# Other parts for the last weights, f16 halves and an f16 selector for the slots' output, low centroid sums in PSUM, and all steps in another sequence

## The chip, the cores and the metric

One core of a Trainium2 chip runs the whole program. The metric is the device time of one execution in microseconds (us). A core has TensorE (matmuls and their weight loads), VectorE, ScalarE, GpSimd, and SyncE, whose queue issues most of the DMAs. In the profile these are PE and PEld, DVE, ACT, POOL and SP.

## The reference

Three stages in one launch, with results in float32 (w_in and w_out come in with 64 bits a value):

```
# 1. clustered attention: batch 2, 8 heads, 768 positions, head size 64, 16 clusters
q_assign = argmax(normalised q . normalised centroids);  k_assign likewise
scores = where(q_assign == k_assign, q @ k.T / 8, -1e9)
attn_out = softmax(scores) @ v                     # -> x: 1536 tokens x 512
# 2. a dense layer
h = x @ w_in                                       # 512 -> 2048
x = (h * clip(h + 3, 0, 6) / 6) @ w_out            # 2048 -> 512
# 3. soft mixture of experts: 8 experts, 4 slots each
logits = x @ phi                                   # 1536 x 32
slot_input = softmax(logits, over tokens).T @ x    # 32 x 512
slot_out[e] = relu(slot_input[e] @ w1[e]) @ w2[e]  # w1: 512 x 1024, w2: 1024 x 512
out = softmax(logits, over slots) @ slot_out       # 1536 x 512
```

w1 and w2 are 8 x 2 MB each, 32 MB that are read once.

## The kernel before, in words

**Steps.** The kernel is a list of 1178 small generators ("events"): each `yield` ends a step. The string `ORDER` is a list of event numbers; `flush` takes one step of an event for each number, and so writes the instruction stream of every engine. The program text fixes which steps there are, `ORDER` alone fixes their sequence on each engine and in each DMA queue. The string `ROOMS` gives many tiles the number of their buffer, in PSUM and SBUF.

**Attention.** For each of the 16 heads (`HEADS`): `load` brings q, k and v; `cast_hi` and `cast_lo` split q and k into f16 halves (high, and what is left, low) in one buffer that all heads share, and a transpose DMA turns them; `as_mm` multiplies with the high and low halves of the centroids (`ct`), adds both sums and begins the arg-max, `as_max` ends it, `as_put` puts the one-hot rows beside q and k; `maxq`, `maxr` and `shift` find each row's maximum; `scores`, `exps`, `plow` and `pv` make the weighted sums, and `finish` divides. `cnt_mm` is for clusters without keys. The halves of a product are summed in PSUM, so that f16 matmuls give float32 accuracy. For head 0 the turning is done by TensorE.

**Weights of the dense layer.** w_in and w_out come as 16 loads of 512 KB each (`win_load`, `wout_load`) in a wider format (64 bits a value), and are narrowed in place (`narrow`: two instructions on VectorE, L912 and L916, one on ScalarE) and then split. w_out is folded with phi (`wphi1` to `wphi3`) and written back to DRAM for the end.

**Dense layer.** `hid`, `act`, `logits`, `colmax`, `dweights` and `dispatch` run for 12 tiles of 128 tokens; those of the first batch lie between the attention heads of the second. At the end `zsum`, `slot_in` and `slot_t` make the slots' inputs.

**Experts.** `fetch` brings w1 and w2 in chunks of 1 MB, in the order of `chunks`, each into the room that `rooms` names; a room comes free when its last reader is done, and a load in SP's queue waits for that, with all behind it. `layer1`, `relu`, `turn` and `layer2` work on groups of four experts, of which each has 32 columns of TensorE. The second layer of the last group is made in two `PARTS` of the 512 output columns (`layer2_part`), so that the first part can go out while the weights of the second come: 384 columns and then 128. Their chunks are of kind "d". `slots_out` takes the 4 rows of each expert out of the group results (`o2s`, float32, copied from PSUM) with a selector matrix `sel` in float32, built by 24 small GpSimd copies, and splits the sum into f16 halves (`s16`); `combine` multiplies with the softmax weights, scales and writes out, in six DMAs for the first part and two for the second.

**Keep.** `keep` issues matmuls (L377) whose result nobody reads; 136 of them lie where TensorE would stand still.

## Time and profile before

| | us |
|---|---|
| median of 3 runs | 449.64 (448.59 to 452.29) |
| the profiled execution | 451.0 |
| its span, first to last instruction | 449.1 |
| TensorE busy | 429.5 (96% of the span) |
| ScalarE, VectorE, GpSimd busy | 309.8, 274.9, 251.1 |
| granted TensorE clock, mean | 0.991 |

Times below are us from the start of the span. Busy time of TensorE counts "keep" matmuls too, and matmuls that overlap in its pipeline.

### The profile page before, as it was taken

The page shows a single profiled execution, that of the slowest core. Times are in us where ns is not written, and L with a number is a line of the kernel's source. Part 1 is how long each engine was busy: PE and PEld are TensorE (multiplying, and loading weights), DVE is VectorE, ACT ScalarE, POOL GpSimd, SP SyncE. Part 2 cuts the span into 40 slices and gives each one's busy share as a digit, 9 for nine tenths or more (in the row PEclk, how much of TensorE's full clock was granted, in tenths as well). Part 3 has the DMA queues.
Part 4 walks back from the last instruction along what each step waited for, and adds up shares of the span by engine and source line. Part 5 has one row for each costly group of instructions (what it writes and reads, how often), then busy time and mean ns, then how long its engine had stood idle before and what let it go on. Part 6 is the DMA issues. An engine that isn't in the chain of part 4 may idle for free.

```text
span 449.1 us, 11732 instructions
## 1 busy us (share of the span) xinstructions
PE 429.5 (96%) x4866; PEld 276.1 (61%) x4866; DVE 274.9 (61%) x479; ACT 309.8 (69%) x508; POOL 251.1 (56%) x229
## 2 busy tenths in 40 slices
PE   8899999999999999999999999999999999889983
PEld 6567778777886556565656567774555445623432
DVE  5989999999866686484666577513434225540322
ACT  7789999988999887888778789874344344501112
POOL 6557588965665676678759788884232333130000
PEclk9999999999999999999999999999999999989997
DMA  8999958997677998407664719907996888799978
GB/s 268 250 201 221 262 89 230 232 234 257 223 173 108 273 260 190 140 14 153 131 165 86 175 22 341 227 14 143 290 393 183 200 216 273 249 378 347 382 211 278
DMA packets 126645, 95.23 MB, mean 212 GB/s; under 512 B 95360, under 2 KB 111744, under 8 KB 126592
## 3 DMA queue, kind: packets, MB, share of 16 engines
q1 hardware_dynamic: 122672, 88.69, 75.1%
q10 hardware_dynamic: 3920, 5.80, 3.6%
q8 instruction: 38, 0.62, 0.6%
q14 instruction: 15, 0.12, 0.1%
HBM read 64.06 MB, written 7.34 MB: 159 GB/s over the span
## 4 chain that ended last, share of the span: by engine, by line
PE 73%; DVE 11%; DMA 6%; ACT 5%; issue 2%; POOL 1%; SPq 0%; DVEq 0%; ACTq 0%; POOLq 0%
PE h L745 27%; PE st L591 5%; PE sm L553 5%; PE st L595 5%; DVE mxs L569 4%; PE acc L661 4%; PE acc L674 3%; DMA wk<-in_moe_w_dram 2%; PE acc L667 2%; PE acc L666 2%; DMA pr<-in_moe_w_dram 2%; PE z L853 2%; PE kw L377 2%; PE lg L796 2%; DMA qk1t<-pr 1%
## 5 line engine op out<-in xcount | busy, mean ns | idle before, releaser
L368 POOL TENSOR_TENSOR pp<-p,pp 128x768 f16<-128x768 f32 x72 | 118.4, 1653 | 46.6 <-ACT pp L358 31.7
L745 PE MATMUL h<-wq,xt 128*128 128x512 f16 x576 | 134.1, 379 | 0.0
L569 DVE TENSOR_REDUCE mxs<-sm 128x1 f32<-128x768 f32 x96 | 89.1, 951 | 20.7 <-PE sm L553 19.9
L745 PEld LDWEIGHTS <-xt 128*128 128x128 f16 x576 | 54.4, 98 | 59.4 <-issue 2.1
L368 POOL TENSOR_TENSOR ghl<-r,ghl 128x1024 f16<-128x1024 f32 (+1 forms) x25 | 50.3, 2014 | 59.1 <-ACT ghl L358 54.6
L639 ACT ACTIVATE p<-st 128x768 f32<-128x768 f32 x72 | 58.2, 811 | 18.3 <-PE st L595 14.4
L358 ACT ACTIVATE pp<-p 128x768 f16<-128x768 f32 x72 | 60.4, 842 | 2.8 <-PE acc L674 1.8
L764 DVE SCALAR_TENSOR_TENSOR r<-r,h 128x1024 f32<-128x1024 f32 (+1 forms) x26 | 29.5, 1137 | 28.6 <-ACT r L762 28.3
L762 ACT ACTIVATE r<-h,b_relu 128x1024 f32<-128x1024 f32 (+1 forms) x26 | 27.1, 1047 | 17.6 <-POOL ghl L368 9.4
L591 PE MATMUL st<-qk1t 128*128 128x384 f16 x144 | 35.1, 325 | 2.3 <-DVE qk2t L578 0.7
L358 ACT ACTIVATE ghl<-r 128x1024 f16<-128x1024 f32 (+1 forms) x26 | 25.5, 986 | 16.1 <-PE z L853 8.4
L667 PE MATMUL acc<-v,pp 128*128 128x64 f16 x432 | 36.1, 194 | 0.0
L666 PE MATMUL acc<-v,pp 128*128 128x65 f16 x432 | 36.1, 192 | 0.0
L661 PE MATMUL acc<-v,pp 128*128 128x65 f32 x288 | 35.6, 273 | 0.0
L661 PEld LDWEIGHTS acc<-v,pp 128*128 128x128 f32 x288 | 34.7, 192 | 0.9
L595 PE MATMUL st<-qk2t 102*128 102x384 f16 x144 | 35.2, 325 | 0.0
L553 PE MATMUL sm<-qk2t 80*128 80x384 f16 x144 | 34.4, 325 | 0.7 <-ACT wot L989 0.2
L666 PEld LDWEIGHTS <-pp 128*128 128x128 f16 x432 | 31.5, 99 | 2.9
L368 POOL TENSOR_TENSOR pr<-pr,pr 128x768 f16<-128x768 f32 x15 | 25.2, 1677 | 13.6 <-ACT pr L358 10.3
L667 PEld LDWEIGHTS <-pp 128*128 128x128 f16 x432 | 29.2, 96 | 2.8
L358 ACT ACTIVATE pr<-pr 128x768 f32<-128x768 f32 (+2 forms) x32 | 26.3, 823 | 4.0 <-DMA qk1t<-pr 2.2
L377 PE MATMUL kw<-ident,ident 128*128 128x256 f16 x136 | 22.9, 294 | 2.6 <-POOL b_relu L870 1.7
(223 smaller groups left out, 801.7 us busy)
## 6 DMA issues: line engine op xcount, KB each, us to landing
wk<-in_moe_w_dram SPq DMA_DIRECT2D x36, 512.0 KB, 6.7
wi<-in_moe_w_in_dram SPq DMA_DIRECT2D x16, 512.0 KB, 6.2
wod<-in_moe_w_out_dram SPq DMA_DIRECT2D x16, 512.0 KB, 4.8
pr<-in_moe_w_dram SPq DMA_DIRECT2D x12, 512.0 KB, 6.5
wos<-wo ACTq DMA_DIRECT2D x8, 512.0 KB, 3.3
wk<-wos SPq DMA_DIRECT2D x8, 512.0 KB, 5.1
pr<-in_q_dram SPq DMA_DIRECT2D x16, 192.0 KB, 4.4
pr<-in_k_dram SPq DMA_DIRECT2D x16, 192.0 KB, 4.3
```

The source lines that it names most:

```text
L358: nc.scalar.activation(out, in_, AF.Copy, scale=scale)
L368: (nc.vector if e == "v" else nc.gpsimd).tensor_tensor(out=out, in0=in_, in1=hi, op=ALU.subtract)
L377: nc.tensor.matmul(t[:, 0, 0:256], ident16, ident.bitcast(F16), start=True, stop=True)
L553: nc.tensor.matmul(s[:, j, 0:384], d["qk2t"][0:80, n, 0], d["qk2t"][0:80, 3 * j : 3 * j + 3, 1], start=True, stop=True,)
L569: nc.vector.tensor_reduce(out=mxs[i % 2][:, 96 + n : 97 + n], in_=s[:, :, 0:384], op=ALU.max, axis=AX.XY)
L591: nc.tensor.matmul(s[:, j, 0:384], d["qk1t"][:, t, 1], d["qk1t"][:, 3 * j : 3 * j + 3, 0], start=True, stop=False)
L595: nc.tensor.matmul(s[:, j, 0:384], d["qk2t"][0 : 96 + NT, t, 1], d["qk2t"][0 : 96 + NT, 3 * j : 3 * j + 3, 0], start=False, stop=True,)
L639: nc.scalar.activation(p32, s[:, :, 0:384], AF.Exp, scale=sc_exp)
L661: nc.tensor.matmul(o, p32[:, j, r * P : (r + 1) * P], d["v32"][:, t], start=(t == 0 and n == 0), stop=False)
L666: nc.tensor.matmul(o, hi, v1[:, t, 0:65], start=(t == 0 and n == 0), stop=False)
L667: nc.tensor.matmul(o[:, 0:64], hi, v1[:, t, 65:129], start=False, stop=False)
L745: nc.tensor.matmul(s[:, fb % 2], xt[:, lhs], wq[fb][:, hl, kk], start=(n == 0), stop=(n == 11))
```

## The change

There are five edits:

- `as_mm`: for heads 0 and 1 the sums with the low centroids are added in PSUM by 24 matmuls of 16 columns, in place of 12 of 32 columns, a copy on ScalarE and an add on VectorE. The other 14 heads stay as they were.
- `PARTS`: 352 and 160 columns in place of 384 and 128. The chunks "d" are cut anew: for each of the four experts four loads of two rows of 352 columns each for part 0, in two chunks, and two of four rows of 160 columns for part 1; all loads of part 1 stand behind all of part 0.
- The group results leave PSUM as two f16 halves (`o2_halves`: the high one by ScalarE, the low one by VectorE), scaled by a mask of each group's rows; the selector is f16, made by one GpSimd copy of `i4`.
- `slots_out` multiplies the high halves into rows 0 to 64 and the low ones into rows 64 to 96, and the two copies of the result are one of ScalarE and one of VectorE.
- `ORDER` and `ROOMS` are new throughout. The loads of w_in and the steps on them stand at other places; the warm-up of the Exp table (`second`) stands later; fourteen `keep` events stand behind the last `act` where eight stood before.

The diff, without the strings of `ORDER` and `ROOMS`, of which 179 lines are changed:

```diff
--- before.py
+++ after.py
@@ -27,179 +27,179 @@
 ORDER = (
-    "0 837 807 9 811 8 9 809 0 15 15 803 829 840 0 0 0 16 16 16 16 16 5 10 8 11 13 13 842 848 834 820 8 8 16 16 8 "
...
+    "9 0 9 822 838 13 836 8 0 810 811 15 15 1124 8 823 7 13 12 12 16 16 842 16 16 8 63 16 110 829 16 837 0 832 16 "
...
@@ -463,21 +463,29 @@
         d = st[i]
         pm = psm(f"as_{i}")
         a2 = pm[:, 0 : 24 * C].rearrange("p (n l c) -> p n l c", l=2, c=C)
+        a = a2[:, :, 0]
         for n in range(2 * NT):
-            nc.tensor.matmul(
-                a2[:, n],
-                d["qk1t"][:, n // 2, n % 2],
-                ct[:, :, h * C : (h + 1) * C],
-                start=(n == 0),
-                stop=(n == 2 * NT - 1),
-            )
-        yield
-        a = a2[:, :, 0]
-        ac = sm.tile([P, 12, C], F32, tag="ac", name=f"ac_{i}", bufs=1)
-        nc.scalar.copy(ac, a2[:, :, 1])
-        yield
-        nc.vector.tensor_tensor(out=a, in0=a, in1=ac, op=ALU.add)
-        yield
+            x = d["qk1t"][:, n // 2, n % 2]
+            if i < 2:
+                for l in range(2):
+                    nc.tensor.matmul(
+                        a[:, n],
+                        x,
+                        ct[:, l, h * C : (h + 1) * C],
+                        start=(n == 0 and l == 0),
+                        stop=(n == 2 * NT - 1 and l == 1),
+                    )
+            else:
+                nc.tensor.matmul(
+                    a2[:, n], x, ct[:, :, h * C : (h + 1) * C], start=(n == 0), stop=(n == 2 * NT - 1)
+                )
+        yield
+        if i >= 2:
+            ac = sm.tile([P, 12, C], F32, tag="ac", name=f"ac_{i}", bufs=1)
+            nc.scalar.copy(ac, a2[:, :, 1])
+            yield
+            nc.vector.tensor_tensor(out=a, in0=a, in1=ac, op=ALU.add)
+            yield
         mx = sm.tile([P, 12], F32, tag="mx", name=f"mx_{i}", bufs=2)
         nc.vector.tensor_reduce(out=mx, in_=a, op=ALU.max, axis=AX.X)
         nc.vector.tensor_tensor(out=a, in0=a, in1=mx.unsqueeze(2).to_broadcast([P, 12, C]), op=ALU.is_equal)
@@ -1014,7 +1022,7 @@
 
 
     NG = E // 4
-    PARTS = [(0, 384), (384, 128)]
+    PARTS = [(0, 352), (352, 160)]
     chunks = [("o", c, 0) for c in range(4)]
     chunks += [("1", 4 * g + j, hf) for g in range(NG) for hf in range(2) for j in range(4)]
     chunks += [("2", 4 * g + j, hf) for g in range(NG - 1) for hf in range(2) for j in range(4)]
@@ -1042,40 +1050,22 @@
         n = ring["n"]
         ring["n"] += 1
         kind, e, hf = chunks[n]
-        if kind == "d" and hf == 1:
-
+        if kind == "d":
             ts = []
-            for j in range(4):
+            for j in range(4 if hf else 1):
                 t = room(n + j, rooms[n + j], 2048, f"wk_{n + j}")
-                u = t[:, 0:1152].rearrange("p (c d) -> p c d", c=3)
-                v = t[:, 1152:2048].rearrange("p (c d) -> p c d", c=7)
-                for c in range(1, 8):
-                    wd[e + j, 1, c] = v[:, c - 1]
-                for c in range(5, 8):
-                    wd[e + j, 0, c] = u[:, c - 5]
-                ts.append((u, v))
-            for j in range(4):
+                for p, (c0, w) in enumerate(PARTS):
+                    u = wd[e + j, p, hf] = t[:, 4 * c0 : 4 * c0 + 4 * w].rearrange("p (c d) -> p c d", c=4)
+                    for c in range(4):
+                        wd[e + j, p, 4 * hf + c, "w"] = u[:, c]
+            todo = [(0, hf, r, 2, j) for r in (0, 2) for j in range(4 if hf else 1)]
+            if hf:
+                todo += [(1, f, 0, 4, j) for f in range(2) for j in range(4)]
+            for p, f, r, m, j in todo:
+                c0, w = PARTS[p]
                 src = w2[e + j].rearrange("(p c) d -> p c d", c=8)
-                nc.sync.dma_start(ts[j][0], src[:, 5:8, 0:384])
+                nc.sync.dma_start(wd[e + j, p, f][:, r : r + m], src[:, 4 * f + r : 4 * f + r + m, c0 : c0 + w])
                 yield
-            for lo, hi in ((1, 4), (4, 8)):
-                for j in range(4):
-                    src = w2[e + j].rearrange("(p c) d -> p c d", c=8)
-                    nc.sync.dma_start(ts[j][1][:, lo - 1 : hi - 1], src[:, lo:hi, 384:512])
-                    yield
-            return
-        if kind == "d":
-            src = w2[e].rearrange("(p c) d -> p c d", c=8)
-            t = room(n, rooms[n], 2048, f"wk_{n}")
-            u = t[:, 512:2048].rearrange("p (c d) -> p c d", c=4)
-            wd[e, 0, 0] = t[:, 0:384]
-            wd[e, 1, 0] = t[:, 384:512]
-            for c in range(1, 5):
-                wd[e, 0, c] = u[:, c - 1]
-            nc.sync.dma_start(u, src[:, 1:5, 0:384])
-            yield
-            nc.sync.dma_start(t[:, 0:512], src[:, 0])
-            yield
             return
         if kind == "1":
             src = w1[e].rearrange("(p k) f -> p k f", k=4)[:, 2 * hf : 2 * hf + 2]
@@ -1338,38 +1328,42 @@
         nc.vector.tensor_copy(cT, tp)
 
     def selectors():
-        sel = sl["sel"] = lt2k("a1", 0, [NG, 3, NS], F32)
-        nc.gpsimd.memset(sel, 0.0)
-        yield
-        for g in range(NG):
-            for j in range(4):
-                for i3 in range(3):
-                    c0 = 16 * g + 4 * j
-                    nc.gpsimd.tensor_copy(
-                        sel[32 * j : 32 * j + 32, g, i3, c0 : c0 + 4],
-                        ident[32 * j : 32 * j + 32, 32 * j + c0 : 32 * j + c0 + 4],
-                    )
-            yield
-
+        sel = sl["sel"] = lt2k("a1", 0, [3, NS], F16)
+        nc.gpsimd.tensor_copy(sel, i4.unsqueeze(1).to_broadcast([P, 3, NS]))
+        yield
+        m = sl["mask"] = sm.tile([P, NG], F32, tag="mx2", name="mask", bufs=2)
+        for j in range(4):
+            b = ident[32 * j : 32 * j + 32, 32 * j : 32 * j + 32].rearrange("p (g j i) -> p g j i", g=NG, j=4)
+            nc.vector.tensor_reduce(out=m[32 * j : 32 * j + 32], in_=b[:, :, j], op=ALU.add, axis=AX.X)
+        yield
+        nc.vector.tensor_scalar(out=m, in0=m, scalar1=SO, scalar2=None, op0=ALU.mult)
+
+    def o2_halves(g, c0, w, src):
+        if ("o2s", g) not in sl:
+            sl["o2s", g] = lt2k("w1", g, [2, 512], F16)
+        hi, lo = (sl["o2s", g][:, a, c0 : c0 + w] for a in range(2))
+        m = sl["mask"][:, g : g + 1]
+        nc.scalar.activation(hi, src, AF.Identity, scale=m)
+        yield
+        nc.vector.scalar_tensor_tensor(out=lo, in0=src, scalar=m, in1=hi, op0=ALU.mult, op1=ALU.subtract)
 
     def slots_out(p):
         c0, w = PARTS[p]
         so = sl["so", p] = psm(f"so_{p}")
-        for g in range(NG):
-            nc.tensor.matmul(
-                so[0:96, 0:w],
-                sl["sel"][:, g].rearrange("p a s -> p (a s)"),
-                sl["o2s", g][:, c0 : c0 + w],
-                start=(g == 0),
-                stop=(g == NG - 1),
-            )
-        yield
+        sel = sl["sel"].rearrange("p a s -> p (a s)")
         s16 = sl["s16", p] = lt2k("a1", 1 + p, [512], F16)[:, 0:w]
-        nc.scalar.activation(s16[0:96], so[0:96, 0:w], AF.Copy, scale=SO)
-        yield
-        nc.vector.scalar_tensor_tensor(
-            out=s16[64:96], in0=so[64:96, 0:w], scalar=SO, in1=s16[64:96], op0=ALU.mult, op1=ALU.subtract
-        )
+        for a, (r0, r1) in enumerate(((0, 64), (64, 96))):
+            for g in range(NG):
+                nc.tensor.matmul(
+                    so[r0:r1, 0:w],
+                    sel[:, r0:r1],
+                    sl["o2s", g][:, a, c0 : c0 + w],
+                    start=(g == 0),
+                    stop=(g == NG - 1),
+                )
+                yield
+            (nc.vector.tensor_copy if a else nc.scalar.copy)(s16[r0:r1], so[r0:r1, 0:w])
+            yield
 
     def combine(p, b):
         c0, w = PARTS[p]
@@ -1458,9 +1452,7 @@
         yield
 
     def store2(g):
-        sl["o2s", g] = lt2k("w1", g, [512], F32)
-        nc.vector.tensor_copy(sl["o2s", g], sl["o2", g])
-        yield
+        yield from o2_halves(g, 0, 512, sl["o2", g])
 
     def layer2_part(p, i):
         c0, w = PARTS[p]
@@ -1471,15 +1463,14 @@
                 nc.tensor.matmul(
                     sl["o2", NG - 1, p][32 * j : 32 * j + 32, 0:w],
                     hw(NG - 1, c, j),
-                    wd[E - 4 + j, p, c],
+                    wd[E - 4 + j, p, c, "w"],
                     start=(c == 0),
                     stop=(c == 7),
                 )
-        yield
+            if c % 2:
+                yield
         if i:
-            if p == 0:
-                sl["o2s", NG - 1] = lt2k("w1", NG - 1, [512], F32)
-            nc.vector.tensor_copy(sl["o2s", NG - 1][:, c0 : c0 + w], sl["o2", NG - 1, p][:, 0:w])
+            yield from o2_halves(NG - 1, c0, w, sl["o2", NG - 1, p][:, 0:w])
 
     for n in range(14):
         ev(keep, 47 + n, 2)
```

## Rows read from the trace of the kernel before

**Rows 1.** Stretches: busy time and instructions by engine, clock, DMA share, GB/s
```profile
0.00:30.00 30.00, 26.03 (x235) 18.18 (x236) 22.66 (x50) 23.37 (x41) 16.50 (x55) 1.00 0.93 240
30.00:105.00 75.00, 73.25 (x921) 59.40 (x920) 71.30 (x114) 70.37 (x108) 55.57 (x38) 1.00 0.91 222
105.00:370.00 265.00, 263.38 (x2991) 166.00 (x2990) 152.59 (x263) 197.48 (x316) 169.37 (x107) 1.00 0.72 179
370.00:390.00 20.00, 18.56 (x239) 11.95 (x237) 12.46 (x24) 11.15 (x29) 5.56 (x4) 1.00 0.78 252
390.00:435.00 45.00, 41.89 (x415) 16.43 (x418) 11.06 (x24) 3.95 (x9) 4.06 (x26) 0.96 1.00 348
```

**Rows 2.** The same view, of the keep matmuls (L377) alone
```profile
0.00:30.00 30.00, 16.30 (x98) 10.17 (x98) 1.00 0.93 240
30.00:370.00 340.00, 2.67 (x14) 1.16 (x14) 1.00 0.76 189
```

**Rows 3.** Timeline near the start, ACT, DVE, SP, PE: start, duration, instruction, idle before
```profile
8.70 0.32 ACT L477 COPY ac<-as 128x192 f32<-128x192 f32 x1 [0.85 <-PE as L467]
8.92 0.85 ACT L358 ACTIVATE pr<-pr 128x768 f16<-128x768 f32 x1
...
9.06 0.37 DVE L479 TENSOR_TENSOR as<-as,ac 128x192 f32<-128x192 f32 x1 [0.89 <-ACT ac L477]
...
11.52 1.85 SPq L443 DMA_TRANSPOSE qk1t<-pr  x1
...
18.55 2.17 SPq L443 DMA_TRANSPOSE qk1t<-pr  x1
...
22.97 0.96 DVE L578 SCALAR_TENSOR_TENSOR pr<-sm,nident 6x768 f16<-6x768 f32 x1
...
24.87 0.47 PE L467 MATMUL as<-ct,qk1t 128*128 128x32 f16 x12 [0.64 <-DMA qk1t<-pr]
```

**Rows 4.** Stretches between the input and the output stream
```profile
434.00:435.00 1.00, 1.00 (x29) 0.76 (x32) 0.13 (x1) 0.49 (x1) 0.00 (x0) 1.00 0.58 156
435.00:436.00 1.00, 0.85 (x16) 0.47 (x9) 0.42 (x1) 0.00 (x1) 0.00 (x0) 1.00 0.13 32
436.00:437.00 1.00, 0.75 (x5) 0.35 (x4) 0.68 (x1) 0.81 (x1) 0.00 (x0) 1.00 0.00 1
437.00:438.00 1.00, 1.00 (x14) 0.44 (x15) 0.90 (x2) 0.15 (x1) 0.00 (x0) 1.00 0.21 81
...
438.00:447.00 9.00, 3.78 (x60) 2.85 (x50) 2.85 (x6) 2.50 (x5) 0.00 (x0) 0.85 1.02 339
```

**Rows 5.** Timeline of the tail, all engines
```profile
421.11 11.08 SPq L1064 DMA_DIRECT2D wk<-in_moe_w_dram  x8
...
430.59 2.12 PE L1471 MATMUL o<-wk,late_w 128*32 128x384 f32 x18 [0.76 <-DMA wk<-in_moe_w_dram]
...
432.64 0.24 PEld L1359 LDWEIGHTS so<-late_w,late_a 128*96 128x96 f32 x2 [0.62 <-issue]
432.64 1.67 PE L1359 MATMUL so<-late_w,late_a 128*96 128x384 f32 x4
432.75 0.56 DVE L1482 COPY late_w<-o 128x384 f32<-128x384 f32 x1 [6.60 <-PE o L1471]
...
434.35 0.49 ACT L1368 ACTIVATE late_a<-so 96x384 f16<-96x384 f32 x1 [16.85 <-PE so L1359]
...
434.87 0.56 DVE L1370 SCALAR_TENSOR_TENSOR late_a<-so,late_a 32x384 f16<-32x384 f32 x1 [1.56 <-ACT late_a L1368]
...
435.48 1.14 PE L1393 MATMUL po<-late_a,late_a 96*128 96x384 f16 x6 [0.15 <-DVE late_a L1370]
...
436.84 0.91 ACTq L1404 DMA_DIRECT2D out_dram<-late_w  x2
```

**Rows 6.** Groups by line: busy us, mean ns, idle time before them
```profile
L916 DVE SCALAR_TENSOR_TENSOR wi<-nt_i,pr 128x1024 uint32<-128x1024 uint32 x8 | 9.8, 1219 | 0.2
...
L912 DVE TENSOR_SCALAR pr<-wi 128x1024 uint32<-128x1024 uint32 x8 | 8.6, 1069 | 0.1
```

328 rows, old and new, of tables (ORDER, ROOMS) are left out of this document.

## The prediction

> **What bounds the kernel now.** I read the span in five stretches first [rows 1], then the matmuls whose result nobody reads [rows 2], then the timeline of the two ends [rows 3, 5], and the DMA load microsecond by microsecond where the input stream gives way to the output stream [rows 4].
>
> The stretches show four regimes; the reader looks for the engine, or the DMA share, that fills its stretch. From 0 to 30 us TensorE is busy for 26.03 us [rows 1], but 16.30 of these are "keep" matmuls [rows 2]: useful work waits for a chain over ScalarE, VectorE, GpSimd and DMA. From 30 to 105 us both TensorE (73.25 of 75) and VectorE (71.30) are nearly full. From 105 to 390 us TensorE alone is the bound (263.38 of 265, then 18.56 of 20). From 390 to 435 us it is the DMA: its share is 1.00 at 348 GB/s, while the other engines have room. After that comes the output: it runs from 438 to 447 us at 339 GB/s and a share of 1.02 [rows 4]. Between the two streams the DMA load falls to 0.58, 0.13, 0.00 and 0.21 of a microsecond each, so 0.42 + 0.87 + 1.00 + 0.79 = 3.1 us of DMA time pass unused just where DMA is the bound.
>
> The profiled execution took 451.0 us with a span of 449.1; 1.9 us lie outside. It is 1.4 above the median of 449.64, so I work out differences on the profile and put them on the median. Some 1% (4.5 us) is what a measurement of this kernel can tell from no change, since its three runs lie 3.7 us apart.
>
> **Change part by part.**
>
> *Low centroid sums in PSUM, heads 0 and 1.* Removed per head: one ScalarE copy (0.32 us) and one VectorE add (0.37 us) [rows 3]; added: twelve more small matmuls. For head 0 this is on the path: VectorE stands idle 0.89 us until the copy has come, then adds, so the reduction behind it can start 0.89 + 0.37 = 1.26 us earlier; for head 1 VectorE, which is full there, saves another add, taken at the same 0.37. Together 1.6 us off the chain that ends in head 0's shift at 22.97 us. The added matmuls: the twelve of head 2 are one row of 0.47 us; twelve more cost between 0 (narrower ones, 16 columns for 32) and 0.47 us per head. I take 0, since keep matmuls fill that time; without that cover it is 0.5 us.
>
> A second chain ends just behind the first: the high half of head 1 stands on ScalarE behind that same copy (8.70, then 8.92), from it hang GpSimd's low half and the transpose DMA issued at 11.52; head 2 uses the same buffer, its transpose is issued at 18.55, and TensorE's centroid matmuls for head 2 at 24.87, ahead of all scores, wait for it (0.64 us idle in the weight loads just before). Without the copy ScalarE can start head 1's high half some 1.1 us earlier (the cast ahead of it ends about 7.85, worked out as 8.70 less the 0.85 us that ScalarE idles there). So both chains shorten, by 1.1 and 1.6 us. In SP's queue the old order at the start is q, k, v of head 0, q and k of head 1, four W_in loads; the new one is q and k of both heads, two W_in loads, q of head 2, v of head 0, two W_in loads. Every W_in load of 512 KB that is passed brings head 1's operands no later than before; v of head 0 is late by two such loads, and nothing reads it before head 0's first weighted sum. I take **-1.6 us**, with ends 0 (VectorE gives it back before 105 us, below) and -2.5 (head 1's cast also passes ahead of the transposed copies).
>
> *The Exp table is warmed later*, behind the first steps on W_in. If those functions need a load of their own, ScalarE pays one more; it has 30 - 23.37 us free in the first stretch [rows 1], and I take 0.
>
> *Parts of 352 and 160 columns.* The second part's weights grow from 7 of 8 rows of 128 columns (4 x 7 x 128 x 128 x 4 B = 1.84 MB behind the last load of part 0) to 8 of 160 (2.62 MB). The last byte of part 0 so lies 0.79 MB earlier in the stream: 2.3 us at 348 GB/s [rows 1]. Part 0 is what TensorE waits for: its last 18 matmuls start at 430.59 [rows 5]. The total of bytes is the same. The run length of a row goes from 512 B to 640 B in part 1 and from 1536 to 1408 in part 0; the eight old short-run loads take 11.08 us of SP's time from 421.11 on, 1.4 each. More loads of that kind cost up to 0.5 us, longer runs give about as much back: 0.
>
> The Trainium skill, "DMA: Bandwidth & Descriptors", section "Bandwidth", asks for batches of 1 MiB or more; the change cuts the last weights into 24 loads of 0.33 to 0.36 MB where there were 20 of 0.19 to 0.77. The stretch from 390 to 435 us shows no such loss with half-megabyte loads in a full queue. By that page the stream would end later, not earlier.
>
> *f16 halves and an f16 selector.* Old chain in part 0: matmuls from 430.59, VectorE copy 0.56, four f32 selector matmuls 1.67, ScalarE 0.49, VectorE 0.56, first output issue 436.84: 6.25 us [rows 5]. New: ScalarE high half and VectorE low half, where I take ScalarE's 0.49 and VectorE's 0.56 for the same columns; the f16 selector matmuls at the price of the nearest f16 rows (six of 384 columns in 1.14 us, 0.19 each): four are 0.76 at most and two of them stand under the low half, so 0.4; then the two last copies side by side, 0.5. In place of 0.56 + 1.67 + 0.49 + 0.56 = 3.28 that is 0.49 + 0.56 + 0.4 + 0.5 = 1.95, **1.3 us less**, with ends 0.3 (four in a row, and a stop at each switch) and 1.6. The added wait is VectorE's, for ScalarE's high half; behind it in VectorE's queue stand only the output copies of the same part, which need it anyway. GpSimd loses 24 small copies that nobody waited for: 0.
>
> Weight loads of the selector stand idle 0.62 us after the 32-column matmuls [rows 5]. The skill's "TensorEngine Tiling (Array Packing)", section "Key Properties", says that a switch of tiling mode drains TensorE; this row agrees. The new selector runs in tiles of 64 and 32 rows between layer-2 matmuls. By that rule each part has some two switches more, 1.2 us by the row, and the gain of the selector would be nil.
>
> Sum for the tail: the first output comes 2.3 + 1.3 = 3.6 us earlier, 433.2 in place of 436.84, ahead of the end of the input at 435. The two streams then touch, and the 3.1 us hole closes. More can't be had there: from then on the 9 us of output are late next. Part 1 has its 3 us of chain behind the last input byte, while part 0's output still runs. I take **-2.8 us** (ends +0.6, -3.1).
>
> *The order and the PSUM rooms.* All steps are sequenced anew. What it could win from 30 to 370 us: TensorE's idle 1.75 + 1.62 us [rows 1] and 2.67 of keeps [rows 2], 6 us in all; what it could lose has no such limit. The order leaves the stages as they are: heads come in the same sequence, and most steps on W_in and W_out lie within some forty places of the old ones; the first expert loads stand some 85 places earlier, second halves of others up to 300 earlier or later in SP's queue, but ahead of the loads that wait for W_in's room. Behind those waiting loads stand only later weights. I take 0, ends -4 and +4.
>
> Sum: -1.6 - 2.8 = -4.4 us: 446.6 for a profile like the one shown, 445.2 for the median.
>
> **Rivals.** (a) *VectorE keeps the start's gain.* It is 95% busy from 30 to 105 us. If its work is the bound there, only the removed 2 x 0.37 us stay and the end is 449.6 - 0.7 - 2.8 = 446.1. For it: VectorE's share; against: from 105 us it has time to spare and TensorE's backlog is what counts. (b) *The hole moves.* If switches eat the selector's gain and the last loads come 0.6 us later, the hole stays and the end is 449.6 - 1.6 = 448.0. (c) *Slower: a narrowing step of W_in ahead of a shift.* Such a step puts 1.07 and 1.22 us on VectorE [rows 6]; put in ahead of a head's maxima or shift in the full stretch, it makes TensorE wait 2.3 us unless another head's scores are ready. Four such places cost 9.2 us, 449.6 - 4.4 + 9.2 = 454.4; from two on the gain is gone. (d) *The new order also fills the middle:* 4 of the 6 us more, 441.2. (e) The new parts or sums change nothing that ends last: that is (a) and (b) together, 448.9.
>
> **How the numbers follow.** Forecast 0.38 (443.5 to 446); (a) 0.14; (b) and (e) 0.15; (c) 0.12; (d) 0.21. The range leaves out half of (c) and the far end of (d): 440.8 to 451. Faster by over 1% (below 445.1): (d) and six tenths of the forecast, 0.44. Slower by over 1%: 0.1, most of (c). The rest, 0.46, lies within 1%.
>
> **What would show it.** Right: head 0's shift near 21.5 us and the scores' start near 23.3; the DMA share without a hole between input and output; the first output issue about 3.5 us before its old distance from the end of the input stream. Wrong: TensorE idle of more than 5 us from 30 to 370 us (c), VectorE idle there grown by what the start gained (a), or a DMA hole as before (b).

## The result, and the profile after

The changed kernel is slower: 453.42 us at the median of 22 runs against 450.13 for the kernel before in runs beside it, a ratio of 1.0068 with a 95% interval of 1.0052 to 1.0084; 0.68% is 3.1 us. Forecast was 445.2, and 440.8 to 451.0 as range.

The two profiled executions alone would not show this. That of the changed kernel took 451.2 us with a span of 449.1, the same span as before; it is the third fastest of its 22, and its mean granted clock is 0.996; only one other has as much (0.997). Sixteen had 0.991 to 0.993, four 0.984 or 0.985. What a typical execution lacks had to come from other runs.

The stretches of the changed kernel (columns as in [rows 1]):

```profile
0.00:30.00 30.00, 24.31 (x258) 17.62 (x258) 23.05 (x47) 22.93 (x40) 15.22 (x55) 1.00 0.90 242
30.00:105.00 75.00, 73.84 (x927) 59.38 (x926) 70.08 (x119) 71.51 (x111) 57.04 (x40) 1.00 0.95 226
105.00:370.00 265.00, 262.28 (x3009) 165.18 (x3007) 151.81 (x260) 195.78 (x313) 169.03 (x106) 1.00 0.76 176
370.00:390.00 20.00, 18.34 (x215) 11.56 (x212) 12.10 (x25) 11.69 (x32) 5.56 (x4) 1.00 0.82 285
390.00:435.00 45.00, 41.33 (x419) 16.99 (x421) 12.46 (x28) 5.34 (x9) 0.68 (x2) 1.00 1.02 339
```

The reader sees the same four regimes, 1.7 us less TensorE time in the first 30 us, and 339 GB/s in place of 348 where DMA is the bound. From 30 to 370 us TensorE is idle for 1.16 + 2.72 = 3.9 us, 3.4 before [rows 1]: the middle held. At the start the keep matmuls alone are 2.5 us less (the same view, of L377; 16.30 in [rows 2]):

```profile
0.00:30.00 30.00, 13.79 (x90) 9.17 (x90) 1.00 0.90 242
```

The start, from the timeline (start, duration, instruction, idle time before), with the first matmul of zsum, where the experts' part begins:

```profile
7.92 0.76 PE L471 MATMUL as<-ct,pr 128*128 128x16 f16 x24 [0.20 <-ACT pr L419]
...
8.53 1.69 PE L377 MATMUL kw<-ident,ident 128*128 128x256 f16 x14
...
9.50 1.39 DVE L920 TENSOR_SCALAR pr<-wi 128x1024 uint32<-128x1024 uint32 x1 [1.84 <-DMA wi<-in_moe_w_in_dram]
...
10.81 0.35 DVE L490 TENSOR_REDUCE mx<-as 128x12 f32<-128x192 f32 x1
...
13.27 0.83 PE L415 MATMUL tq<-ident,pr 128*128 128x128 f16 x12 [3.05 <-ACT pr L516]
...
23.29 0.96 DVE L586 SCALAR_TENSOR_TENSOR pr<-sm,nident 6x768 f16<-6x768 f32 x1
...
389.14 1.16 PE L1244 MATMUL zt<-nident,zacc 128*128 128x128 f32 x8 [0.18 <-DVE nident L1241]
```

and of the kernel before:

```profile
8.22 0.45 PE L467 MATMUL as<-ct,pr 128*128 128x32 f16 x12
...
9.46 0.36 DVE L482 TENSOR_REDUCE mx<-as 128x12 f32<-128x192 f32 x1
...
390.36 1.16 PE L1254 MATMUL zt<-nident,zacc 128*128 128x128 f32 x8 [0.18 <-DVE nident L1251]
```

The ScalarE copy and the VectorE add of [rows 3] are gone, yet head 0's reduction (L490) starts 2.89 us behind the first centroid matmul (L471), where before it was 1.24 us (L482, L467). A shift of W_in (L920; it moves bits, and is not head 0's shift) stands ahead of it in VectorE's queue and waits for its load. TensorE meanwhile runs out of keep matmuls and is idle for 3.05 us. Head 0's shift comes at 23.29, not near 21.5; before it was 22.97 [rows 3].

At the other end, first where the stream of weights is in layer 1, in stretches of 2 us; before:

```profile
396.00:398.00 2.00, 1.20 (x12) 0.13 (x4) 0.73 (x1) 0.00 (x0) 1.41 (x9) 1.00 0.99 379
398.00:400.00 2.00, 1.47 (x12) 1.12 (x16) 0.76 (x3) 0.00 (x0) 1.52 (x12) 0.99 1.00 389
400.00:402.00 2.00, 2.00 (x16) 0.58 (x12) 1.28 (x4) 0.52 (x1) 0.00 (x0) 0.50 1.02 414
```

and after:

```profile
396.00:398.00 2.00, 1.67 (x14) 1.24 (x14) 0.78 (x2) 0.00 (x0) 0.00 (x0) 1.00 0.95 268
398.00:400.00 2.00, 1.83 (x18) 0.55 (x20) 1.86 (x6) 0.00 (x0) 0.00 (x0) 1.00 0.92 248
400.00:402.00 2.00, 2.00 (x24) 0.65 (x20) 0.70 (x5) 0.00 (x0) 0.00 (x0) 1.00 0.81 305
```

Over these 6 us the new kernel moves 2 x (268 + 248 + 305) kB = 1.64 MB, the old one 2.36. The 0.72 MB take 2.1 us at 348 GB/s [rows 1]. SP's timeline in the changed kernel says why: four loads up to 397.06, then nothing until 400.25, when layer 1 gives back a room; two loads that could have gone out at 397 come behind that, at 404.36 and 405.82 (e8 and e10 below move them).

```profile
391.56 5.50 SPq L1087 DMA_DIRECT2D wk<-in_moe_w_dram  x4
400.25 2.06 SPq L1087 DMA_DIRECT2D pr<-in_moe_w_dram  x3
402.37 1.95 SPq L1067 DMA_DIRECT2D pr<-in_moe_w_dram  x2
404.36 0.70 SPq L1087 DMA_DIRECT2D wk<-in_moe_w_dram  x1
...
405.82 0.74 SPq L1087 DMA_DIRECT2D wk<-in_moe_w_dram  x1
```

Two of SP's waits from 384 to 432 us (us in total, times, longest; `e1b` is layer 1's PSUM tile, `si` that of the slot projection):

```profile
SPq L1087 <- PE e1b L1408: 4.0, 2, 3.2
SPq L1087 <- PE si L1271: 3.2, 1, 3.2
```

The end answers to [rows 4, 5]: the first output goes out at 434.69 instead of 436.84 and the hole ahead of it is closed but for 0.2 us (share 1.07, then 0.80 from 435 to 436), but the DMA engines run dry again at 442.

```profile
434.00:435.00 1.00, 1.00 (x24) 0.68 (x25) 0.80 (x1) 0.67 (x1) 0.00 (x0) 1.00 1.07 293
441.00:442.00 1.00, 0.97 (x13) 0.79 (x11) 0.62 (x2) 0.57 (x1) 0.00 (x0) 1.00 0.72 261
442.00:443.00 1.00, 0.76 (x4) 0.29 (x3) 0.60 (x2) 0.21 (x1) 0.00 (x0) 1.00 0.14 49
443.00:444.00 1.00, 0.00 (x0) 0.00 (x0) 0.00 (x0) 0.36 (x1) 0.00 (x0) 1.00 0.61 194
```

### The profile page after: what moved, and what is told of

It reads as the page before. It is cut to its first block, busy times and chain, and to the rows that moved or that the text cites. A ratio compares the mean times of both kernels' runs of the same rounds, so it can differ in the third digit from the quotient of the medians.

```text
span 449.1 us, 11751 instructions
## 1 busy us (share of the span) xinstructions
PE 426.9 (95%) x4890; PEld 274.7 (61%) x4890; DVE 273.3 (61%) x482; ACT 310.6 (69%) x509; POOL 247.5 (55%) x205
## 4 chain that ended last, share of the span: by engine, by line
PE 56%; DMA 6%; ACT 2%; SPq 2%; DVE 1%; issue 0%; ACTq 0%; DVEq 0%
PE h L753 27%; DMA wk<-in_moe_w_dram 5%; PE st L599 3%; PE st L603 3%; PE sm L561 3%; PE acc L674 2%; PE acc L675 2%; PE acc L682 2%; PE z L861 2%; PE lg L804 2%; SPq L1067 2%; PE gp L790 1%; PE e L1408 1%; PE e1b L1408 1%; DMA qk2t<-pr 1%; PE si L1271 1%
## 5 line engine op out<-in xcount | busy, mean ns | idle before, releaser
L753 PEld LDWEIGHTS <-xt 128*128 128x128 f16 x576 | 54.2, 97 | 59.1 <-issue 2.1
L674 PE MATMUL acc<-v,pp 128*128 128x65 f16 x432 | 36.1, 192 | 0.0
L682 PE MATMUL acc<-v,pp 128*128 128x65 f16 x432 | 24.9, 193 | 0.0
```

Of the source, the lines that this page charges most:

```text
L674: nc.tensor.matmul(o, hi, v1[:, t, 0:65], start=(t == 0 and n == 0), stop=False)
L682: nc.tensor.matmul(o, pl[:, j, r * P : (r + 1) * P], v1[:, t, 0:65], start=False, stop=False)
L753: nc.tensor.matmul(s[:, fb % 2], xt[:, lhs], wq[fb][:, hl, kk], start=(n == 0), stop=(n == 11))
```

## The experiments

Every kernel was timed beside the kernel before on its own chip, so kernels are compared by ratio (1% is 4.5 us). To tell start, middle and end apart, I read two distances from each profile: **A**, from the first centroid matmul of head 0 to the first matmul of zsum, the sum that begins the slots' inputs (which leaves out that the first load lands 2 us sooner or later from execution to execution), and **B**, from there to the end of the span. Ratios come from all timed executions, A and B from the one that was profiled.

| kernel | ratio (95%) | A, us | B, us |
|---|---|---|---|
| before | 1 | 382.1 | 58.8 |
| after | 1.0068 (1.0052 to 1.0084) | 381.2 | 60.0 |
| e1_tail | 1.0035 (1.0017 to 1.0052) | 381.8 | 58.8 |
| e2_head | 1.0018 (0.9996 to 1.0040) | 380.3 | 56.5 |
| e3_sums | 1.0021 (0.9995 to 1.0046) | 382.4 | 57.3 |
| e4_parts384 | 1.0079 (1.0051 to 1.0108) | 381.4 | 59.1 |
| e5_fill | 1.0147 (1.0125 to 1.0169) | 382.9 | 63.6 |
| e6_tail_fill | 1.0119 (1.0103 to 1.0134) | 381.7 | 62.6 |
| e7_again | one run: 451.8 us | 380.5 | 60.0 |
| e8_ahead | 1.0046 (1.0025 to 1.0067) | 382.7 | 58.9 |
| e9_keeps | 1.0097 (1.0081 to 1.0113) | 382.6 | 60.1 |
| e10_tail_ahead | 0.9986 (0.9973 to 0.9999) | 381.3 | 56.6 |
| e11_both | 1.0028 (1.0007 to 1.0050) | 381.0 | 59.4 |
| e12_keeps_start | 1.0062 (1.0040 to 1.0084) | 381.3 | 60.8 |
| e13_three | 0.9972 (0.9956 to 0.9989) | 380.6 | 57.1 |
| e14_rooms | 1.0036 (1.0017 to 1.0055) | 381.5 | 59.1 |
| e15_head_keeps | 0.9981 (0.9956 to 1.0006) | 381.6 | 57.1 |
| e16_three_parts384 | 0.9989 (0.9971 to 1.0007) | 381.2 | 58.7 |
| e17_four | 0.9972 (0.9953 to 0.9992) | 380.3 | 55.7 |
| e18_win_late | 1.0043 (1.0017 to 1.0070) | 380.8 | 59.1 |

### Which part loses: e1 to e4

Four kernels, each with one part of the change. In the diffs the order is written in step names, and they are cut to the lines that matter.

```diff
 e1_tail: the order of before up to zsum, the changed code and order behind it
 e2_head: the changed order and as_mm up to zsum, the old code and order behind it
 e3_sums: before, with as_mm of after (its extra matmuls too) for heads 0 and 1
+        if i >= 2:
             ac = sm.tile([P, 12, C], F32, tag="ac", name=f"ac_{i}", bufs=1)
             nc.scalar.copy(ac, a2[:, :, 1])
 e4_parts384: after, with
-    PARTS = [(0, 352), (352, 160)]
+    PARTS = [(0, 384), (384, 128)]
```

> The old sequence up to the slots' sums (zsum), then the changed tail alone: f16 halves and selector, parts of 352 and 160 columns, their loads, and the new sequence from there on. Theory T (the tail loses: part 1 now has 2.62 MB of short runs, its last weights land 2 to 3 us later, and a new hole in the DMA load opens behind them): 1 to 3.5 us slower than before. Theory O (the new sequence ahead of the tail loses, the tail gains what was forecast): 2 to 3 us faster than before.

> The new sequence and the low centroid sums in PSUM up to the slots' sums, then the old tail with 384 and 128 columns and the float32 selector. Theory T: 1 to 2 us faster than before, which is the earlier start of the slots' sums in the profile of the changed kernel (389.14 in place of 390.36). Theory O: 2 to 5 us slower than before.

> The kernel before with one edit: for heads 0 and 1 the low centroid sums are added in PSUM; every other step keeps its place. If the start's chain is what the forecast took it for: 1 to 1.6 us faster. If VectorE or TensorE give it back before the tail, or the tail's stream of loads does not follow the start: within 0.5 us of before.

> The changed kernel with parts of 384 and 128 columns again (its loads cut the new way: four rows of 128 columns, 2.10 MB, behind the last load of part 0), all else as changed. Theory T: the last weights land earlier, 1 to 2.5 us faster than the changed kernel, so within 1.5 us of before. Theory O: no faster than the changed kernel, 3 to 5 us slower than before.

The low sums alone gain nothing (e3: 1.0021, A 382.4 against 382.1). The new tail alone loses 0.35% (e1). The new head alone gains nothing at the median (e2), though its profile, the fastest of its 12 executions, has an A of 380.3. Taking back the column split does not help (e4). In B the four stand apart: the old tail takes 56.5 to 57.3 us in e2 and e3 (in the profile of before, 58.8 with the clock at 0.50 from 400 to 403), the new one 58.8 to 60.0.

### First theory of the tail, which fell: e5, e6

The new split puts 704 KB into each room that comes free in layer 1 where the old loads put 1 MB. I took that for the cause of the dry stretch.

```diff
             for p, f, r, m, j in todo:
...
-                nc.sync.dma_start(wd[e + j, p, f][:, r : r + m], src[:, 4 * f + r : 4 * f + r + m, c0 : c0 + w])
+                if not (hf and p and f == 0):
+                    nc.sync.dma_start(wd[e + j, p, f][:, r : r + m], src[:, 4 * f + r : 4 * f + r + m, c0 : c0 + w])
+                if not hf and r == 2:
+                    c0, w = PARTS[1]
+                    nc.sync.dma_start(wd[e + j, 1, 0], src[:, 0:4, c0 : c0 + w])
                 yield
```

> The changed kernel, except that each of the four rooms that come free during layer 1 (the d chunks with half 0) takes part 1's columns of its four chunks (320 KB) right behind the second load of part 0, where the changed kernel loads them at the very end of the stream. Theory (the new split leaves the freed rooms 1.25 MB short, so the DMA engines run dry while they wait for rooms: 248 to 305 GB/s over 396 to 404 us in the changed kernel against 358 to 412 with the old split, 0.9 MB or 2.4 us): the rate over 396 to 404 comes back to 350 or more, the last weight lands 1.5 to 2.5 us earlier against the start of zsum, the span from zsum's first matmul to the end falls from 60.0 to 57.5 to 58.5 us, and the median falls by 1.5 to 2.5 us against the changed kernel's 453.4, to about 451.5. Rival (the stream's end is set by the number and run length of part 1's loads): the rate may rise at 400, but the last weight and the end stay within 0.5 us, median 453 to 453.5. Second rival (the rooms come free later in the new order, whatever is put into them): the dip in the rate stays.

> The same edit in e1_tail, which has the old head and the new tail (450.49 us, ratio 1.0035 to before; 58.9 us from zsum to the end, with 260 and 244 GB/s over 400 to 404 us against 408 and 358 for the old tail). Theory of the short rooms: 0.5 MB or 1.4 us of the dry stretch come back, the span from zsum's first matmul to the end falls to 57 to 58 us, median about 449.2, ratio 0.998 to 1.001. Rival (number and run length of part 1's loads): 450.3 to 450.7.

Both are some 4 us slower than their base. The dry stretch did not fill, it deepened; part 0's weights came later, TensorE stood idle, and what followed ran at half clock. Stretches of e6_tail_fill:

```profile
400.00:402.00 2.00, 2.00 (x24) 0.56 (x20) 0.98 (x5) 0.00 (x0) 0.00 (x0) 1.00 0.44 111
...
422.00:424.00 2.00, 0.00 (x0) 0.00 (x0) 0.00 (x0) 0.00 (x0) 0.00 (x0) 1.00 1.13 360
424.00:426.00 2.00, 1.66 (x12) 0.60 (x16) 0.00 (x0) 0.00 (x0) 0.00 (x0) 0.55 1.02 372
```

More bytes per room are no cure: in e6 SP issues nothing from 396.6 to 400.5, as before the edit. That the size of a load is not the cause either is shown by e13 below, which has the same sizes and no dry stretch. The rival of rooms that come free late, whatever is put in, is the one that stands.

### What SP waits for: e7 to e10

e7 is the changed kernel once more; it again caught an execution at a clock of 0.997 (451.8 us, B 60.0), so it says only that B repeats. SP's order shows two ready loads, the second halves (512 KB each) of chunks 24 and 25 of layer 2, behind three loads that wait for layer 1. e8 moves the two in the changed kernel, e10 in e1_tail. e9 tests a rival for the typical execution, a fall of the clock behind TensorE's wait for weights at 421 us.

```diff
 e8_ahead, e10_tail_ahead
-fetch 25.0, fetch 26.0, 27.0, 27.1, 28.0, 29.0, fetch 25.1, 28.1, turn, fetch 24.1, 30.0
+fetch 25.0, fetch 24.1, fetch 25.1, fetch 26.0, 27.0, 27.1, 28.0, 29.0, 28.1, turn, 30.0
 e9_keeps
-layer2_part 0,0 (first half), layer2_part 0,0 (second half)
+layer2_part 0,0 (first half), 4 x keep of two matmuls, layer2_part 0,0 (second half)
```

> The changed kernel once more, for a second profile: 16 of its 22 executions had a mean granted clock of 0.991 to 0.993 and took 453.4 us at the median, while the profiled one had 0.996 and took 451.2. If a stretch at the lower clock is what makes the typical execution longer, a profile at 0.99 shows a stretch below 1.00 of 3 to 4 us that the first profile does not have, and the time lost, 2 us, lies in that stretch; if it is the middle that varies, the start of zsum is later at full clock.

> The changed kernel with two steps moved: the second halves (512 KB each) of chunks 24 and 25 of layer 2 are issued right behind their first halves, ahead of the three loads that wait for layer 1 to give their rooms back; in the changed kernel they stand behind those loads in SP's queue, though their rooms are free. Theory (ready loads stuck behind waiting ones): the trace of the changed kernel has 8 loads issued between 387.3 and 397.1 us and the next at 400.25, the old tail has 10; with 10 the rate over 396 to 404 rises from 248 to 305 GB/s to 360 or more, the weights that TensorE waits for at 421 land 1.5 to 2.5 us earlier, the wait of 1.2 us there goes, the span from zsum's first matmul to the end falls from 60.0 to about 58 us, and the median from 453.4 to 450 to 451.5 us, with the mean granted clock at 0.995 or more in most executions. Rival (number and size of the loads of part 1, eight of 320 KB at 312 GB/s): the rate at 400 rises, but the end stays within 0.5 us: 453 to 453.5. Rival (typical executions are long for a clock that falls whatever the stream does): a median of 452.5 to 453.

> The changed kernel with eight more idle matmuls of 256 columns (1.3 us) on TensorE just ahead of the matmuls of part 0 that wait for weights at 421 us (1.22 us in the profile); nothing else is changed, the loads least of all. If typical executions of the changed kernel are 2.2 us longer than the profiled one since the clock falls after that wait, and layer 2 behind it runs at half speed, the idle matmuls keep the clock up: median 451 to 452, mean granted clock mostly 0.996. If the clock falls elsewhere or costs nothing, the median stays at 453 to 454.

> The same move of two steps in e1_tail (old head, new tail; 450.49 us, ratio 1.0035; 58.9 us from zsum to the end, 260 and 244 GB/s over 400 to 404 us). Theory of the stuck loads: the dry stretch closes, 57.3 to 58 us from zsum to the end, median 449 to 449.7, ratio 0.998 to 1.001. Rival (loads of part 1): 450.3 to 450.8.

With the old head the move gives back everything: e10 against e1 is 0.9986 against 1.0035, 2.2 us, and B falls by 2.3 to 56.6. With the new head it gives 1.1 us of B and 0.22% of the ratio, which the intervals do not separate from nothing; over 396 to 402 us the rate rises only from 274 to 315 GB/s, so something else still holds the stream up there. The keeps of e9 ran where they should (at 422.13) and changed nothing for the better. But its profile and that of e8 have the clock of most executions (0.991 and 0.993), and show where it falls. Stretches of e8_ahead:

```profile
12.00:14.00 2.00, 0.85 (x9) 0.89 (x10) 1.78 (x3) 1.00 (x4) 0.92 (x1) 0.79 1.48 221
14.00:16.00 2.00, 2.00 (x14) 1.43 (x12) 1.16 (x2) 2.00 (x3) 0.00 (x0) 0.50 0.92 221
16.00:18.00 2.00, 1.94 (x12) 1.17 (x11) 1.39 (x2) 1.92 (x3) 0.00 (x0) 0.86 1.05 380
```

It falls to 0.50 (1.2 GHz) right behind the idle stretch at the start (2.74 us there), while the profile of the changed kernel, with 3.05 us idle, has 1.00 there. e5, e8 and e9 have this fall and an A of 382.6 to 382.9; the ten other profiles with the new head up to e16, which have no fall, have 380.3 to 381.6 and 381.1 as their mean: 1.7 us. Some 1 us of it is there already at head 0's shift, 16.3 to 16.5 us behind the first centroid matmul in the three, 15.4 in the ten.

### The start and the rooms: e11 to e15

The second thing that holds the stream up is another wait in the same place. SP waits for the slot projection (si) to give back rooms: 3.2 us at once in the changed kernel (above), in two waits of 1.7 at most in e1_tail:

```profile
SPq L1083 <- PE si L1267: 3.2, 2, 1.7
```

In ROOMS, chunks 24 and 25 stand in the rooms of the third and fourth chunk of the slot projection's weights; with the old head in e1 they fall on the first and the fourth.

```diff
 e12_keeps_start, e11_both (with the move of e8), e15_head_keeps (in e2_head)
-keep 9, cast_lo 1
+keep 9, 10 x keep of two matmuls, cast_lo 1
 e14_rooms, e13_three (with the move of e8 and the keeps)
-wk_24:0 wk_25:2 late_a0:1 late_a1:3
+wk_24:1 wk_25:3 late_a0:0 late_a1:2
```

> The changed kernel with two edits: the move of e8_ahead (two ready loads ahead of the three waiting ones) and 20 more idle matmuls (2.2 us) behind the 14 that stand at 8.5 us, where TensorE of the changed kernel is idle from 10.2 to 13.3 us. Theory (the changed kernel loses in two places: ready loads stuck behind waiting ones, 2.7 us; a clock of half speed from 13.4 to 16.7 us in most executions, after an idle stretch of 3 us that 26 idle matmuls cover in the kernel before, 2 us or so): the two add up, zsum's first matmul starts by 389.2 us, the median is 448 to 449, mean granted clock mostly 0.995 or more, ratio to before 0.994 to 1.000. Rival (the clock at the start costs nothing, since VectorE and DMA set the start): as e8_ahead, 450.7.

> The changed kernel with only the 20 more idle matmuls at 10.2 us. Theory of the clock at the start: granted clock 1.00 from 12 to 20 us, mean clock mostly 0.995 or more (0.991 to 0.993 in 16 of 22 executions of the changed kernel), median 451 to 451.8 instead of 453.4. Rival (the clock at the start costs nothing): 453 to 453.8, at a higher mean clock. Rival (the idle matmuls are late themselves and push the transposes behind them): slower than 453.4.

> e11_both (two ready loads ahead, 20 more idle matmuls at the start) with chunks 24 and 25 in the rooms of the first two chunks of the slot projection instead of the last two (the two late tiles that stood there go to the other rooms). Theory (late rooms: SP stands still from 391.8 to 395.4 us, and the stream has a gap at 398): the load issued at 395.4 moves to 393 to 394, the rate over 396 to 402 rises from 290 to 370 GB/s or more, 57 us from zsum's first matmul to the end, median 447.3 to 448.5. Rival (something else in the new head, as the place of the late tiles or the chunk that is loaded last, slows the stream): 450 to 451, as e11_both.

> The changed kernel with the change of rooms alone: chunks 24 and 25 take the rooms of the first two chunks of the slot projection. Theory of the late rooms: 1 to 2.5 us of the changed kernel's 453.4, so 451 to 452.4; less than in e13_three, since the two stuck loads still leave the stream dry at 400. Rival: 453 to 453.8.

> e2_head (new head, old tail; 450.05 us, but 446.6 to 447.3 in two executions at a clock of 0.996, and 8 of 12 at 0.984 to 0.992) with the 20 more idle matmuls at 10.2 us. If the fall of the clock at 13 us is what keeps the new head's 2 us from showing at the median, the clock is 0.995 or more mostly and the median 447 to 448.5, ratio to before 0.995 to 0.998. If not, 449.5 to 450.5.

The keeps do what they are for to the clock: 1.00 from 12 to 18 us, a mean of 0.995 or more in nine of twelve executions of e12 (two of 22 of the changed kernel). The time does not show it: e12 is at 1.0062 against 1.0068, where 0.35 to 0.5% less was expected, and e11 at 1.0028 against e8's 1.0046, both within the intervals. e15 gains most, 0.9981 against e2's 1.0018, but only five of its twelve executions have 0.995 or more (four of e2's), so this gain is not shown to be that of the clock at the start. The rooms alone give 0.32% (e14), not to be told from the move alone. Together, and with the keeps, they give what neither does: e13 is at 0.9972, 0.96% or 4.3 us under the changed kernel, and faster than the kernel before. Between e11 and e13 only the rooms differ: 0.56%, 2.5 us. The move and the rooms without the keeps were not run together. One stretch, of after, e14_rooms, e11_both (move, no rooms) and e13_three (both), one fence each:

```profile
396.00:402.00 6.00, 5.50 (x50) 2.43 (x54) 3.35 (x11) 0.00 (x0) 0.00 (x0) 1.00 0.90 274
```
```profile
396.00:402.00 6.00, 5.50 (x54) 2.43 (x54) 3.35 (x11) 0.00 (x0) 0.26 (x1) 1.00 0.95 373
```
```profile
396.00:402.00 6.00, 5.50 (x50) 2.39 (x50) 3.35 (x11) 0.00 (x0) 0.00 (x0) 1.00 0.93 291
```
```profile
396.00:402.00 6.00, 5.50 (x54) 2.29 (x50) 3.35 (x11) 0.00 (x0) 0.52 (x2) 1.00 1.02 416
```

With one cause mended SP only comes to the other wait sooner: in e14 it waits 5.4 us at once for layer 1 (3.2 in the changed kernel), in e11 still 3.2 us for the slot projection. With both it has issued six loads by 397.14 and the DMA engines do not run dry.

### The split and the start by themselves: e16 to e18

```diff
 e16_three_parts384: e13_three, with
-    PARTS = [(0, 352), (352, 160)]
+    PARTS = [(0, 384), (384, 128)]
 e18_win_late (in after), e17_four (in e13_three, with 4 keeps instead of 10)
-win 0,0 (shift on VectorE), consts2, as_mm 0, ..., as_max 0, as_put 0
+consts2, as_mm 0, ..., as_max 0, win 0,0 (shift on VectorE), as_put 0
```

> e13_three with parts of 384 and 128 columns, all else as there. If the split of 352 and 160 gains what the prediction gave it (the last byte of part 0 2.3 us earlier, and the hole in the output closed), this is 1 to 2.5 us slower than e13_three's 448.25: 449.3 to 450.8. Rival (the hole moves: e13_three has the DMA engines at 0.13 and 0.17 over 440 to 442 us, between the last output of part 0 and the first of part 1, so what part 0 gains part 1 loses): the first output issues 0.7 to 1 us later, the hole ahead of part 1's output is gone, and the time is within 0.5 us of e13_three, 447.8 to 448.7.

> e13_three with the first step on W_in (shift on VectorE, narrowing on ScalarE) behind head 0's maxima, where the kernel before has it, and 8 more idle matmuls instead of 20. Theory (a step that waits for a load stands ahead of ready work): the first reduction of head 0 starts at 8.7 instead of 10.81 us, its transposes on TensorE at 11.3 to 12 instead of 13.27, and zsum's first matmul 0.8 to 2 us earlier than in e13_three (389.8): 388 to 389; median 446.3 to 447.6. Rival (the next stage takes it: VectorE is full from 30 to 105 us, or head 1 and its transposes set the scores' start): zsum within 0.5 us, median 448 to 448.6.

> The changed kernel with this one step moved. TensorE's idle stretch ahead of head 0's transposes shrinks from 3 us to 1 to 1.8, the clock stays up in most executions (0.995 or more), and the median falls from 453.4 by the 1.4 us that the clock costs (e12_keeps_start) and by what the earlier start is worth, 450.5 to 452. Rival (the start sets nothing, only the clock does): 452. Rival (the later steps on W_in push the first scores): 453 or more.

e16 is 0.17% above e13, within the intervals of both: the split is worth 0.8 us by the medians, and anything from nothing to some 1.9 us by the intervals. The first output of e16 comes 45.9 us behind zsum, that of e13 43.0, 2.9 us earlier; 1.5 us of that may be the stream of e16's profiled execution (450.4 us, a long one), whose last weight lands 47.2 us behind zsum against 45.7. Part 0 so gains 1.4 to 2.9 us by the split. Part 1 gives most of it back, as the stretches of e13_three show between the last output of part 0 and the first of part 1 (a hole of 3.1 us in [rows 4], here one of 1.7 us):

```profile
434.00:440.00 6.00, 4.36 (x59) 2.78 (x57) 2.71 (x5) 2.62 (x5) 0.00 (x0) 1.00 0.97 343
440.00:442.00 2.00, 1.14 (x9) 0.48 (x6) 1.01 (x2) 0.71 (x2) 0.00 (x0) 1.00 0.15 48
442.00:445.00 3.00, 0.00 (x0) 0.00 (x0) 0.00 (x0) 0.00 (x0) 0.00 (x0) 0.98 1.00 307
```

Besides this hole e13 leaves 0.7 us of DMA time unused from 433 to 435 (shares 0.53 and 0.77), 2.4 us in all; e16 leaves 2.2 (0.17 and 0.33 from 435 to 437, 0.27 from 443 to 444). So in these two profiles the split moves unused DMA time and does not lessen it.

In e17 and e18 head 0's transposes follow its centroid matmuls by 3.3 us instead of 5.35. Head 0's shift gains 0.7 of these 2.0 us (14.7 us behind the same matmuls against 15.4), and the time of e17 is that of e13. e18 is 0.25% under the changed kernel, within the intervals; TensorE's idle stretch there is 1.0 us, and only six of its twelve executions have a clock of 0.995 or more. The rival that the next stage takes it was right in e17.

## Why the prediction was wrong

**The step that failed is the order, put at 0**, and in it the sentence "Behind those waiting loads stand only later weights". It speaks of the loads that wait for W_in's room, and I asked no more of the weights behind them. Among these, two loads that were ready stood behind three that wait for layer 1, and ahead of all five stood the first halves of their chunks, in rooms that the slot projection gives back last. I had weighed the order as places passed in a list; what counts is which semaphore each load in SP's queue waits for and what stands behind it. Its price is the new tail's B: 60.0 us against 57.1 in e13 with the same parts and loads, and 57.3 with the old tail at full clock (e3). In the time, e13 is 4.3 us under the changed kernel; that counts the keep matmuls at the start too. The prediction drew on the rule of the Trainium skill's "DMA: Bandwidth & Descriptors", section "Bandwidth" (batches of 1 MiB or more), by which it had the stream end later for its smaller loads. It does end later, its last load 48.4 us behind zsum against 45.2 in e3; but in e13, with loads of the same sizes, it is 45.7, so the sizes account for 0.5 us at most.

**The start: -1.6 us forecast, none measured.** Without copy and add, head 0's reduction comes 0.78 us behind the first centroid matmul in e3, against 1.24 before: 0.46 us, not 1.26. Some 0.5 of the 0.89 us that VectorE stood idle before the add were a wait for the centroid matmuls themselves (8.22 to 8.67), and that wait stays; and the twelve added matmuls, put at 0, make these 0.3 us longer (0.76 against 0.45). In e3 even this is lost at the next step: the shift of W_in behind the one-hot rows takes 2.02 us where it took 0.68 before, head 0's shift comes at 23.76 us, and A is 382.4 against 382.1. In the changed kernel the step on W_in ahead of the reduction costs 2.1 us (2.89 against 0.78), of which e17 shows 0.7 at head 0's shift and nothing in the time. That is rival (c)'s mechanism, put in the wrong place: not between 30 and 105 us, but at 9.5, behind a load.

**The keep matmuls.** I priced their cover at 0.5 us. They also keep the clock: with 12 fewer of them behind the first centroid matmuls, TensorE's idle stretch there is followed by 1.2 GHz in three profiles, and A is 1.7 us longer in these. That such a fall is what most executions have is argued from their mean clock, which the keeps of e12 raise; that it costs 1.7 us of the time is not shown.

**Parts of 352 and 160.** The first output is 2.2 us earlier in the profile, near the 2.3 us said, but that is luck: 1.2 us of it is an earlier zsum. The last weights of part 0 land 40.2 us behind zsum, no earlier than before (at 429.32, and at 430.55 before), since the dry stretch took what the split gave; in e13 they land 37.6 us behind it. But "Part 1 has its 3 us of chain behind the last input byte, while part 0's output still runs" was wrong: part 0's output ends about 442, part 1's chain takes 4.5 us from its last weight (437.6) to its output (442.11) and outlasts it, and a hole opens there. That is rival (b), without the reasons I gave it.

**The f16 selector: 1.3 us forecast, 0.2 measured.** From TensorE's last matmul of part 0 to the first output it is 430.73 to 434.69, 4.0 us, against 432.71 to 436.84, 4.1 [rows 5]. The rows of the changed kernel:

```profile
429.36 1.37 PE L1463 MATMUL o<-wk,late_w 128*32 128x352 f32 x10 [0.20 <-DMA wk<-in_moe_w_dram]
...
430.66 0.11 PEld L1357 LDWEIGHTS <-late_a 128*64 128x64 f16 x1 [0.57 <-issue]
...
430.77 0.55 ACT L1346 ACTIVATE late_w<-o,mask 128x352 f16<-128x352 f32 x1 [3.08 <-PE o L1463]
...
431.36 0.58 DVE L1348 SCALAR_TENSOR_TENSOR late_w<-o,mask,late_w 128x352 f16<-128x352 f32 x1 [2.89 <-ACT late_w L1346]
...
431.72 0.45 ACT L1365 CAST late_a<-so 64x352 f16<-64x352 f32 x1 [0.40 <-PE so L1357]
431.86 0.95 DVE L1328 COPY late_a<-cTp 128x1536 f16<-128x1536 f16 x1
...
432.21 0.46 PE L1357 MATMUL so<-late_w,late_a 128*32 128x352 f16 x2 [0.21 <-ACT late_a L1365]
...
432.83 0.52 DVE L1365 CAST late_a<-so 32x352 f16<-32x352 f32 x1
...
433.41 1.05 PE L1387 MATMUL po<-late_a,late_a 96*128 96x352 f16 x6 [0.41 <-DVE late_a L1365]
...
434.69 0.91 ACTq L1398 DMA_DIRECT2D out_dram<-late_w  x2
```

The old chain was put too long: I added up instructions that overlap. From the last matmul of part 0 (432.71) to the first matmul of `combine` (435.48) it takes 2.77 us [rows 5], not 3.28, since the first selector matmuls start at 432.64, beside the copy. The new one takes 2.68 us (430.73 to 433.41), not 1.95. The halves cost what was put (0.55 and 0.58), but the low half's matmuls wait for ScalarE's copy of the high rows, until 432.17, though VectorE has their operand ready at 431.94; the pair takes 0.46 us; and VectorE's last copy starts at 432.83, behind a copy of the combine weights (0.95 us) in its queue. The rule on mode switches in the Trainium skill's "TensorEngine Tiling (Array Packing)", section "Key Properties", did not decide: TensorE's weight loads are idle 0.57 us at the first switch, but that lies under the last matmuls, as the 0.62 us before did.

The sum: e13, with the stream mended, is 0.28% (1.3 us) faster than before, not 4.4 us, and the changed kernel is 4.3 us slower than e13. So of the 7.5 us between forecast and result some 4.3 are the order with the keeps at the start, and some 3.1 gains that were not there.

What stays open: why a profile caught the high clock so often in the changed kernel, why 3 us of idle TensorE were followed by the lower clock in one execution and not in another, and why the same shift of W_in takes 0.68 us in one kernel and 2.02 in another.

## What to carry to other kernels

On a queue that issues in order, list for each load the wait that it stands behind: a ready load behind a waiting one leaves the DMA engines short of work, and two such waits in a row hide each other, so that mending one shows little. When an order is changed, check the same for compute queues at the start: a step that waits for a load, placed ahead of ready work, undoes a shortened chain. Before a gain at the end is counted, follow the last part's chain too, since the hole goes to where the next part is late.

## What the runs showed of the hardware

The granted clock fell to 0.50 behind TensorE idle stretches of 2.7 us (e8_ahead) and of 3.15 us (e6_tail_fill, 421.2 to 424.3), for 3.4 us each; in the kernel before it fell at 400 us with no idle stretch of over 0.9 us ahead of it. The idle stretch at the start (3.0 us, 2.7 in e8) was followed by 1.00 in five profiles and by 0.50 in three (e5, e8, e9), so one profile does not tell what a typical execution has. While SP's queue was short of loads, the DMA share stayed near full (0.90 over 396 to 402 us of the changed kernel) at 274 GB/s, and at 1.02 it moved 416 (e13_three): the share by itself did not show that the stream was starved, the rate did.
